# Windowed attention and two MLPs on one core: the second half of the attention taken two rounds at a time, and the weight fold's first blocks moved ahead of the attention's end

## The chip, the cores and the metric

The kernel runs on one core of a Trainium2 chip. The metric is the device time of one execution in microseconds; the lower the better. Three runs of the kernel before gave 868.57 to 869.71 us, with a median of 869.25.

## The reference

```python
def attn(q, k, v):                    # (4 batches, 8 heads, 576 tokens, 64)
    scores = q @ k.transpose(0, 1, 3, 2) / 8
    rel = pos[:, None] - pos[None, :]
    plain   = (rel >= 0) & (rel < 32)                      # heads 0 to 3
    dilated = (rel >= 0) & (rel < 128) & (rel % 4 == 0)    # heads 4 to 7
    return softmax(where(mask, scores, -1e9)) @ v

x = attn(q, k, v) as (2304 tokens, 512)
h = x @ w_in;  x = leaky(h, 0.01) @ w_out                  # 512 -> 2048 -> 512
a, b = x @ w1, x @ w2                                      # 512 -> 1024
out = ((a * b) @ w3) @ w_out2                              # 1024 -> 1024 -> 512
```

q, k and v are float32. The weights arrive as 64-bit floats.

## The kernel before

**Products.** A product of the MLPs is three matmuls (mm3, lines 120 to 122): each operand is held as a high and a low part, and high x high, high x low and low x high are summed in PSUM. A conversion (to_float32, then a split) makes float32 words out of the 64-bit weights first: a scaled copy of the upper words (L107), two on ScalarE (L151, L153), a shift (L141) and an add (L157) on VectorE, then the high part (L110) and the low part (L112).

**MLP 1.** The tokens are cut into seven chunks: two of 320 and 256 tokens for each of batches 0 and 1, then three of 384 for batches 2 and 3 together. A chunk has 16 turns. A turn is one hidden block: 12 matmuls into ps_h (hidden_steps, two PSUM banks in rotation), the leaky step on ScalarE (g, L563), its split (gs: L110 on VectorE, L112 on POOL in the middle chunks) and, two turns later, 12 matmuls into ps_x (project). At the end of a chunk the four accumulators ps_x are copied out to st and stored.

**Attention.** A round is one pair of heads and one part of the tokens, 5 blocks of 64 queries (r = 0) or 4 (r = 1); eight rounds make a batch, 32 in all. A round has these steps: scores (small matmuls into ps_s, L394, then mask, maximum and exponentials, L409 to L418), normalize (L430 to L435), turn_p (transposes into ps_p, L451, copied to pT by ScalarE, L455) and value_steps (small matmuls into ps_o, L472, then copied to x as high and low parts, L500 and L503). For batches 1 to 3 q and k are loaded into "nat" tiles and transposed by VectorE into qT and kT (turn_halves). The tiles ps_s, ps_p and ps_o of the second half share two PSUM banks ("side").

**Order.** Batches 0 and 1 run in an order written out by hand (START). From turn 4 of chunk 2 on, the generator attention() yields steps of rounds 16 to 31, and pace() takes 39/28 of a step in each turn of chunks 2 and 3 and 2.25 in each of the first 13 turns of chunk 4. The text is not the final order: a planner at build time takes, for each engine, the first instruction in the order of the text that its own model holds to be ready. On the chip each engine then runs its list in that order.

**Fold.** w3 and w_out2 are multiplied into one matrix (wp) while MLP 1 goes on. begin_fold, at turn 13 of chunk 4, finishes the attention, closes its pool and opens the pool "fold" in its place; Convert then takes 8 blocks of w_out2 (wo, stored to DRAM) and 16 of w3 (transposed on TensorE, split into w3T), and wp_step makes the products. 1.35 steps of it are taken in each turn from there on. In chunk 6 the blocks of w1 and w2 are converted, and wp is loaded (load_wp) and split. Then come the gates (ps_ab) and the final product (ps_y).

Of the kernel before, what the change touches and what calls it, by code (L numbers as in the profile page):

```python
# [28 lines left out]
def tile_window_attention_two_mlps(  # L29
# [224 lines left out]
    def load_halves(m, src, o):  # L254


        pi, nm = seq[m // 2], "qk"[m % 2]
        t = att.tile([P, NT, D], F32, tag="nat", name=f"{nm}{pi}", bufs=2)
        for g in range(P // E):
            og = o + g // 2 * S * D + g % 2 * E  # L260
            to = t[g * E : (g + 1) * E]
            x = NT * D - E
            nc.sync.dma_start(
                to.rearrange("p n d -> p (n d)")[:, :x], rows(src, og, [[NT * D, E], [1, x]])
            )
        nat_t[nm, pi] = t

    def turn_halves(m):
        pi, nm = seq[m // 2], "qk"[m % 2]
        t = nat_t.pop((nm, pi))  # L270
        dst = att.tile([P, S], F32, tag=nm + "T", name=f"{nm}T{pi}", bufs=2)
        if pair(pi)[2]:
            nc.vector.transpose(dst.rearrange("d (r n) -> d n r", n=NT), t[:, :, :E])
        else:
            for v in range(DILATION):
                us = len(range(v, NT, DILATION))
                other = (NT + v) % DILATION * SR + (NT + v) // DILATION
                to = bass.AP(
                    dst.tensor, dst.offset + v * SR,
                    [list(dst.ap[0]), [1, us], [2 * NT // DILATION, E // 2], [other - v * SR, 2]],  # L280
                )
                at = bass.AP(
                    t.tensor, t.offset + v * D,
                    [list(t.ap[0]), [DILATION * D, us], [2, E // 2], [1, 2]],
                )
                nc.vector.transpose(to, at)
        qk_t[nm, pi] = dst
# [69 lines left out]
    def turn_rows(m):  # L357
        pi, nm = seq[m // 2], "qk"[m % 2]
        plain = pair(pi)[2]
        c = 6 if plain else 8  # L360
        n = S // c
        t = nat_t.pop((nm, pi))
        ps = bank2(f"ps_{nm}T{pi}")
        for g in range(2):
            for c1 in range(c // 2):
                src = t[:n, g * (c // 2) + c1].rearrange("p j d -> p (j d)")
                nc.tensor.transpose(ps[:, g, c1 * n : (c1 + 1) * n], src, ident[:n, :n])
        yield
        dst = att.tile([P, S], F32, tag=nm + "T", name=f"{nm}T{pi}", bufs=2)
        if plain:  # L370
            to = dst.rearrange("d (p g c) -> d g c p", g=2, p=n)
        else:
            to = dst.rearrange("d (c p g) -> d g c p", g=2, p=n)
        copy_on(engine_of[TURN_ON[m]])(to, ps[:, :, : S // 2].rearrange("d g (c p) -> d g c p", p=n))
        qk_t[nm, pi] = dst
        yield
# [134 lines left out]
    def attention(n0, n1):  # L511

        for m in range(n0, n0 + 4):
            transpose_qk(m)
            load_qk(m + 2)
            if m % 2:
                yield
        load_v(n0 // 2 + 1)
        scores(n0)
        yield  # L520
        scores(n0 + 1)
        normalize(n0)
        yield
        for n in range(n0, n1):
            run(turn_p(n))
            normalize(n + 1)
            yield
            if n % 8 != 3:
                scores(n + 2)
                yield  # L530
            transpose_qk(n + 4)
            load_qk(n + 6)
            yield
            if n % 8 == 3:
                scores(n + 2)
                yield
            run(value_steps(n))
            m = n // NA * 4
            if n % NA in (2, 3):
                load_v(m + n % NA)  # L540
            elif n % NA in (5, 7):
                load_v(m + 4 + (n % NA == 7))
            yield


# [119 lines left out]
    def keep_w3(i):  # L665


        def finish(w, e_hi, e_lo):
            ps = bank(f"ps_w3T{i}")
            for j in range(2):  # L670
                for c in range(NG):
                    nc.tensor.transpose(
                        ps[:, (j * NG + c) * P : (j * NG + c + 1) * P],
                        w[:, (c * 2 + j) * P : (c * 2 + j + 1) * P], ident,
                    )
            t = fold.tile([P, 2, 2, NG * P], F32R, tag="w3T", name=f"w3T{i}", bufs=2)
            split(t[:, 0], t[:, 1], ps.rearrange("p (j r) -> p j r", j=2), e_hi, nc.vector)
            w3T.extend((i // (NI // NG), i % (NI // NG) * 2 + j, t[:, :, j]) for j in range(2))

        return finish  # L680

# [23 lines left out]
    wpf = {}  # L705

    def load_wp(ib):
        t = late.tile([P, DM], F32, tag="wpf", name=f"wpf{ib}", bufs=1)
        nc.sync.dma_start(t, wp_dram[ib * P : (ib + 1) * P, :])
        wpf[ib] = t  # L710

# [54 lines left out]

    with ExitStack():
        make_identity(nc, ident)
        att_es, att = pool("att", "right")
        mask_d = masks = att.tile([P, S // QB, KB], BF16, name="masks")  # L770
        nc.vector.memset(masks, 0.0)
        def build_masks():
# [29 lines left out]

        raw_es, rawp = pool("raw", "left")
        homes = {
            "K": (rawp, "kr", 2), "W": (woB_p, "woB", NF // 2), "N": (att, "nat", 2), "V": (att, "v", 2)
        }
        RAW_AT = "WWWWWWWWWWWWWWWWWWWWWWWWNWNWNWNW"
        PAIR_AT = "KKVVKKVVKKVVKKVVKKVVKKVKVKVKVKVK"
# [100 lines left out]
                project(*todo.pop(0))  # L909

        LATE = (4, 13)
        FOLD_PACE = 1.35
        wo2_turn = [0]

# [14 lines left out]
        stream = attention(2 * NA, NR)  # L929
        owed = [0.0]  # L930

        def begin_fold():
            step(*[stream] * 200)
            att_es.close()
            nonlocal fold, fold_es, conv3
            fold_es, fold = pool("fold", "right")
            jobs = [(load_rows, w_out2, jb, keep_wo2(jb)) for jb in range(NI)]
            jobs += [(load_w3, w3, i, keep_w3(i)) for i in range(NI * NI // NG // 2)]

            def fold_tile(tag, dt, bufs):  # L940
                return lambda i: fold.tile([P, 512], dt, tag=tag, name=f"{tag}f{i}", bufs=bufs)

            conv3 = Convert(
                jobs, fold_tile("raw", U64, 2), fold_tile("w", I32, 2), fold_tile("r", I32, 2),
                FOLD_CONV,
            )
            conv3.fetch(2)

        def pace(c):

            owed[0] += 39 / 28 if c < LATE[0] else 2.25
            while owed[0] >= 1:
                owed[0] -= 1
                step(stream)
# [4 lines left out]
        for c, f0, f1 in runs:  # L959
            if first >= f1 - f0:  # L960
                first -= f1 - f0
                continue
            f0, first, f00 = f0 + first, 0, f0
            if c == NCH - 1:
                while conv3.made < len(conv3.jobs) or conv3.done or w3T:
                    fold_step()
                fold_es.close()
                first_es, first_y = pool("first", "right")
                late_es, late = pool("late", "right")

                def raw_last(i):
                    return late.tile([P, 512], U64, tag="raw", name=f"raww{i}", bufs=2)

                wr = {}

                def w_slot(i):
                    wr[i] = late.tile([P, 2, 512], I32, tag="wr", name=f"wr{i}", bufs=2)
                    return wr[i][:, 0]

                jobs = [  # L980
                    (load_cols, (w1, w2)[m], i, keep_cols(w12, (m, i), f"w{m + 1}_{i}"))
                    for i in range(NI)
                    for m in range(2)
                ]
                conv = Convert(jobs, raw_last, w_slot, lambda i: wr[i][:, 1], LAST_CONV)
                conv.fetch(2)
                load_y(0)
            for f in range(f0, f1):
                turn += 1
                mlp1(c, f, f00, f1)  # L990
                if (c, f) == LATE:
                    begin_fold()
                if (c, f) < LATE:
                    pace(c)
                elif c < NCH - 1:
                    owed[0] += FOLD_PACE
                    while owed[0] >= 1:
                        owed[0] -= 1
                        fold_step()
                lagged()  # L1000
                if c == NCH - 1:
                    conv.step()
                    if 2 <= f < 2 + NI:
                        load_wp(f - 2)
                    if 3 <= f < 3 + NI:
                        split_wp(f - 3)
                    if 11 <= f < 11 + NC:
                        split_y(0, f - 11)
# [57 lines left out]
```

## Time and profile before

| | us |
|---|---|
| median of three runs | 869.25 |
| lowest and highest run | 868.57, 869.71 |
| the profiled execution | 868.56 |
| span of its instructions | 866.6 |
| TensorE (PE) busy | 848.2 |
| VectorE (DVE) busy | 346.7 |
| ScalarE (ACT) busy | 352.6 |
| GpSimd (POOL) busy | 210.8 |

The profiled execution lies 1.96 us above its span, and 0.69 us below the median. "Busy" is the time in which an engine executes; PE's matmuls overlap one another, so PE can be busy all the time and still work below its best rate. The distance from one matmul's start to the next one's tells what a matmul costs.

### The profile page before, as it was taken

How to read it: one execution, taken by the hardware profiler on the slowest of the kernel's cores; microseconds unless marked ns; L12 is line 12 of the kernel's file. 1: busy time of each engine (PE TensorE's matmuls, PEld its weight loads, DVE VectorE, ACT ScalarE, POOL GpSimd, SP SyncE). 2: the span in 40 equal slices, each digit the busy share in tenths (PEclk: the TensorE clock that was granted, in tenths of full speed). 3: DMA queues.
4: the chain of work that ended last, by engine and by line, in shares of the span. 5: the costliest groups of instructions: out<-in, count | busy, mean ns of one | idle time of the engine just before them, and what ended most of it. 6: DMA issues, size and time to landing. Idle time of an engine off the chain costs nothing.

```text
span 866.6 us, 14693 instructions
## 1 busy us (share of the span) xinstructions
PE 848.2 (98%) x5774; PEld 772.0 (89%) x5774; DVE 346.7 (40%) x704; ACT 352.6 (41%) x879; POOL 210.8 (24%) x236
## 2 busy tenths in 40 slices
PE   7999998999999999999999999999999999999998
PEld 7799997999999999989899999998888888888887
DVE  4999976344453432274434177731021011000000
ACT  4999945223443343364433175632131121111111
POOL 3311101122322232263222134223123112111110
PEclk9999999999999999999999999999999999999999
DMA  6976575183333311189887575341001000000001
GB/s 152 309 214 231 179 169 137 34 193 73 82 98 92 78 45 50 47 294 349 300 289 236 165 239 155 113 135 49 25 1 61 24 13 13 25 12 13 25 13 48
DMA packets 87333, 103.58 MB, mean 120 GB/s; under 512 B 42849, under 2 KB 65633, under 8 KB 87265
## 3 DMA queue, kind: packets, MB, share of 16 engines
q1 hardware_dynamic: 87264, 102.65, 39.0%
q8 instruction: 45, 0.74, 0.4%
q14 instruction: 24, 0.19, 0.1%
HBM read 85.72 MB, written 16.91 MB: 118 GB/s over the span
## 4 chain that ended last, share of the span: by engine, by line
PE 77%; DMA 7%; DVE 6%; ACT 5%; issue 4%; POOL 2%; SPq 0%; POOLq 0%; DVEq 0%; ACTq 0%
PE ps_ab L120 7%; PE ps_ab L122 7%; PE ps_ab L121 7%; PE ps_x L120 6%; PE ps_x L122 5%; PE ps_x L121 5%; PE ps_h L120 5%; PE ps_h L122 5%; PE ps_h L121 5%; PE ps_y L122 4%; PE ps_y L121 4%; PE ps_y L120 4%; PE ps_s L394 2%; PE ps_o L472 2%; PE ps_wp L122 2%
## 5 line engine op out<-in xcount | busy, mean ns | idle before, releaser
L120 PE MATMUL ps_h<-x,win 128*128 128x384 f32 (+2 forms) x448 | 142.5, 318 | 4.9 <-ACT g L563 4.2
L122 PE MATMUL ps_h<-x,win 128*128 128x384 f32 (+2 forms) x448 | 140.7, 314 | 0.0
L121 PE MATMUL ps_h<-x,win 128*128 128x384 f32 (+2 forms) x448 | 140.4, 313 | 0.0
L120 PE MATMUL ps_x<-gs,wout 128*128 128x384 f32 (+2 forms) x368 | 119.0, 325 | 0.0
L743 DVE TENSOR_TENSOR ab<-a,ps_ab 128x512 f32<-128x512 f32 (+1 forms) x40 | 25.2, 633 | 233.3 <-ACT a L741 225.8
L120 PE MATMUL ps_ab<-ys,w 128*128 128x512 f32 (+1 forms) x320 | 117.7, 368 | 0.6 <-DVE ab L743 0.6
L121 PE MATMUL ps_x<-gs,wout 128*128 128x384 f32 (+2 forms) x368 | 117.7, 320 | 0.1
L122 PE MATMUL ps_ab<-ys,w 128*128 128x512 f32 (+1 forms) x320 | 117.7, 368 | 0.0
L121 PE MATMUL ps_ab<-ys,w 128*128 128x512 f32 (+1 forms) x320 | 117.6, 368 | 0.0
L122 PE MATMUL ps_x<-gs,wout 128*128 128x384 f32 (+2 forms) x368 | 117.4, 319 | 0.0
L112 POOL TENSOR_TENSOR p<-ab,p 128x512 fp32r<-128x512 f32 (+1 forms) x40 | 47.0, 1177 | 211.3 <-ACT p L110 211.3
L110 DVE CAST gs<-g 128x384 fp32r<-128x384 f32 (+2 forms) x92 | 41.3, 449 | 128.9 <-ACT g L563 103.3
L120 PEld LDWEIGHTS ps_h<-x,win 128*128 128x128 f32 x448 | 84.8, 189 | 8.2 <-ACT g L563 6.1
L112 POOL TENSOR_TENSOR gs<-g,gs 128x384 fp32r<-128x384 f32 (+2 forms) x64 | 59.5, 929 | 133.5 <-DVE gs L110 133.5
L563 ACT ACTIVATE g<-ps_h 128x384 f32<-128x384 f32 (+2 forms) x112 | 49.1, 439 | 96.8 <-PE ps_h L122 80.2
L121 PEld LDWEIGHTS ps_h<-x,win 128*128 128x128 f32 x448 | 84.9, 190 | 0.3
L122 PEld LDWEIGHTS ps_h<-x,win 128*128 128x128 f32 x448 | 84.8, 189 | 0.4
L741 ACT COPY a<-ps_ab 128x512 f32<-128x512 f32 (+1 forms) x40 | 21.6, 543 | 139.5 <-PE ps_ab L122 139.5
L120 PEld LDWEIGHTS ps_x<-gs,wout 128*128 128x128 f32 x368 | 69.5, 189 | 1.7
L121 PEld LDWEIGHTS ps_x<-gs,wout 128*128 128x128 f32 x368 | 69.7, 189 | 1.3 <-POOL gs L112 0.4
L122 PEld LDWEIGHTS ps_x<-gs,wout 128*128 128x128 f32 x368 | 69.7, 189 | 0.6
L120 PEld LDWEIGHTS ps_ab<-ys,w 128*128 128x128 f32 x320 | 60.1, 188 | 11.1 <-DVE ab L743 1.0
(109 smaller groups left out, 1553.1 us busy)
## 6 DMA issues: line engine op xcount, KB each, us to landing
wo<-wo_dram SPq DMA_DIRECT2D x32, 512.0 KB
raw<-in_moe_w_in_dram SPq DMA_DIRECT2D x16, 512.0 KB
raw<-in_moe_w_out_dram SPq DMA_DIRECT2D x16, 512.0 KB
rawf<-in_moe_w_dram SPq DMA_DIRECT2D x16, 512.0 KB
raww<-in_moe_w_dram SPq DMA_DIRECT2D x16, 512.0 KB
q<-in_q_dram SPq DMA_DIRECT2D x48, 140.0 KB
k<-in_k_dram SPq DMA_DIRECT2D x48, 140.0 KB
v<-in_v_dram SPq DMA_DIRECT2D x60, 96.0 KB
```

What stands on the lines that cost most here:

```text
L110: copy_on(e_hi)(hi, src)
L112: e_lo.tensor_tensor(lo, src, hi.bitcast(F32), op=ALU.subtract)
L120: nc.tensor.matmul(ps, a[1], b[0], start=first, stop=False)
L121: nc.tensor.matmul(ps, a[0], b[1], start=False, stop=False)
L122: nc.tensor.matmul(ps, a[0], b[0], start=False, stop=last)
L394: nc.tensor.matmul(ps[j * QB : (j + 1) * QB, i - bl.start], qt[d, i * QB : (i + 1) * QB], kt[d, first_key(i, plain) : first_key(i, plain) ...
L472: nc.tensor.matmul(ps[j * D : (j + 1) * D, i * QB : (i + 1) * QB], vt[i][:, h + j, :], t[:, i, j * QB : (j + 1) * QB], start=True, stop=True,)
L563: nc.scalar.activation(g, ps, AF.Prelu, alpha=SLOPE)
L741: nc.scalar.copy(t, ps[0][:, :n])
L743: nc.vector.tensor_tensor(g, t, ps[1][:, :n], op=ALU.mult)
```

## The change

Rounds 16 to 31 are taken in pairs. attention() issues turn_p of round n, then turn_p of round n+1 with the transposes and loads of two q and k tiles, then value_steps of both rounds, then scores and normalize of the next two. There are 36 steps in place of 68, and pace() takes 22/28 and 14/13 of a step per turn in place of 39/28 and 2.25. The loads of v move to the same places of the pairs.

The q and k tiles (nat, qT, kT) get a pool of their own, "qk", that stays open after the attention. The fold's 64-bit words, scaled words and halves take the slots of nat, qT and kT. Its Convert is set up at turn 10 of chunk 4 (CONV_AT), where the first two blocks are asked for, and its first step is taken at turn 13 ahead of begin_fold. The tile w3T is cut in two, each half with its own split, in three buffers of half the size. The tile wpf has two buffers.

```diff
-        t = att.tile([P, NT, D], F32, tag="nat", ...)
+        t = qkp.tile([P, NT, D], F32, tag="nat", ...)      # qT and kT too
...
-        scores(n0)
-        yield
-        scores(n0 + 1)
-        normalize(n0)
-        yield
-        for n in range(n0, n1):
+        for n in (n0, n0 + 1):
+            scores(n)
+        yield
+        for n in (n0, n0 + 1):
+            normalize(n)
+        yield
+        for n in range(n0, n1, 2):
             run(turn_p(n))
-            normalize(n + 1)
             yield
-            if n % 8 != 3:
-                scores(n + 2)
-                yield
-            transpose_qk(n + 4)
-            load_qk(n + 6)
+            run(turn_p(n + 1))
+            turn = [lambda m=m: (transpose_qk(m), load_qk(m + 2)) for m in (n + 4, n + 5)]
+            if n % NA != 4:
+                for f in turn:
+                    f()
             yield
-            if n % 8 == 3:
-                scores(n + 2)
-                yield
-            run(value_steps(n))
+            for i in (n, n + 1):
+                run(value_steps(i))
             m = n // NA * 4
-            if n % NA in (2, 3):
-                load_v(m + n % NA)
-            elif n % NA in (5, 7):
-                load_v(m + 4 + (n % NA == 7))
+            if n % NA == 2:
+                load_v(m + 2)
+                load_v(m + 3)
+            elif n % NA in (4, 6):
+                load_v(m + 2 + n % NA // 2)
+            yield
+            for i in (n + 2, n + 3):
+                scores(i)
+            if n % NA == 4:
+                for f in turn:
+                    f()
+            for i in (n + 2, n + 3):
+                normalize(i)
             yield
...
-            t = fold.tile([P, 2, 2, NG * P], F32R, tag="w3T", name=f"w3T{i}", bufs=2)
-            split(t[:, 0], t[:, 1], ps.rearrange("p (j r) -> p j r", j=2), e_hi, nc.vector)
-            w3T.extend((i // (NI // NG), i % (NI // NG) * 2 + j, t[:, :, j]) for j in range(2))
+            for j in range(2):
+                t = fold.tile([P, 2, NG * P], F32R, tag="w3T", name=f"w3T{i}_{j}", bufs=3)
+                split(t[:, 0], t[:, 1], ps[:, j * NG * P : (j + 1) * NG * P], e_hi, nc.vector)
+                w3T.append((i // (NI // NG), i % (NI // NG) * 2 + j, t))
...
-        t = late.tile([P, DM], F32, tag="wpf", name=f"wpf{ib}", bufs=1)
+        t = late.tile([P, DM], F32, tag="wpf", name=f"wpf{ib}", bufs=2)
...
+        CONV_AT = (4, 10)
...
+        def begin_conv():
+            nonlocal conv3
...
+            def words(tag, dt):
+                return lambda i: qkp.tile([P, 512], dt, tag=tag, name=f"{tag}f{i}", bufs=2)
+
+            conv3 = Convert(jobs, words("nat", U64), words("qT", I32), words("kT", I32), FOLD_CONV)
+            conv3.fetch(2)
...
-            owed[0] += 39 / 28 if c < LATE[0] else 2.25
+            owed[0] += 22 / 28 if c < LATE[0] else 14 / 13
...
+                if (c, f) == CONV_AT:
+                    begin_conv()
                 if (c, f) == LATE:
+                    conv3.step()
                     begin_fold()
```

## Rows read from the trace of the kernel before

**Rows 1.** Windows: stretch, its length, busy us of each engine, PEclk, DMA share, GB/s
```profile
184.00:363.00 179.00, 179.00 (x1644) 169.05 (x1643) 66.90 (x170) 67.44 (x254) 50.38 (x59) 1.00 0.30 76
392.00:500.00 108.00, 107.88 (x581) 98.64 (x580) 40.24 (x68) 39.62 (x68) 25.42 (x30) 1.00 0.78 267
```
**Rows 2.** Timeline of PE: two short bursts among the matmuls of MLP 1
```profile
237.91 0.28 PE L122 MATMUL ps_h<-x,win 128*128 128x256 f32 x1
238.12 1.04 PE L394 MATMUL ps_s<-kT,qT 64*64 64x96 f32 x20
...
239.31 0.28 PE L121 MATMUL ps_h<-x,win 128*128 128x256 f32 x1
239.43 0.29 PE L122 MATMUL ps_h<-x,win 128*128 128x256 f32 x1
239.65 0.69 PE L472 MATMUL ps_o<-pT,v 96*64 96x64 f32 x16
240.26 0.39 PE L120 MATMUL ps_x<-gs,wout 128*128 128x256 f32 x1
240.48 0.28 PE L121 MATMUL ps_x<-gs,wout 128*128 128x256 f32 x1
```
**Rows 3.** Timeline of PE: two rounds' scores in one burst; a longer value burst
```profile
177.50 0.31 PE L122 MATMUL ps_x<-gs,wout 128*128 128x320 f32 x1
177.74 1.54 PE L394 MATMUL ps_s<-kT,qT 64*64 64x96 f32 x32
...
179.46 0.31 PE L121 MATMUL ps_x<-gs,wout 128*128 128x320 f32 x1
179.60 0.31 PE L122 MATMUL ps_x<-gs,wout 128*128 128x320 f32 x1
...
250.62 0.80 PE L472 MATMUL ps_o<-pT,v 96*64 96x64 f32 x20
251.35 0.53 PE L451 MATMUL ps_p<-ident,s 128*96 128x128 f32 x3
```
**Rows 4.** Groups of PE by shape, 184 to 363 us: the scores
```profile
L394 PE MATMUL ps_s<-kT,qT 64*64 64x96 f32 x288 | 15.4, 248 | 0.0
```
**Rows 5.** Timeline of PE where the fold has begun: a wait
```profile
381.87 0.34 PE L122 MATMUL ps_h<-x,win 128*128 128x384 f32 x1
384.26 0.45 PE L120 MATMUL ps_h<-x,win 128*128 128x384 f32 x1 [2.05 <-ACT g L563]
```
**Rows 6.** Windows (columns as in rows 1): right behind that wait
```profile
385.00:390.00 5.00, 5.00 (x22) 5.00 (x21) 4.18 (x6) 2.94 (x6) 3.80 (x4) 0.66 0.95 317
```
**Rows 7.** Timelines of ACT, DVE and POOL ahead of that wait
```profile
381.96 0.62 ACT L110 CAST wo<-wf 128x512 fp32r<-128x512 f32 x1 [2.70 <-DVE wf L157]
...
383.74 0.47 ACT L563 ACTIVATE g<-ps_h 128x384 f32<-128x384 f32 x1
...
377.42 1.22 DVE L110 CAST gs<-g 128x384 fp32r<-128x384 f32 x1 [0.15 <-ACT g L563]
...
379.64 1.24 DVE L141 TENSOR_SCALAR wf<-wf 128x512 int32<-128x512 int32 x1
...
377.08 1.34 POOL L112 TENSOR_TENSOR wo<-wf,wo 128x512 fp32r<-128x512 f32 x1 [1.33 <-ACT wo L110]
```
**Rows 8.** The fold's words: durations in ns (min/median/max), first and last start
```profile
L132 SPq DMA_DIRECT2D rawf<-in_moe_w_out_dram x8: 327/328/433, 340.9 to 380.2; - x8
L141 DVE TENSOR_SCALAR wf<-wf x24: 413/428/1502, 364.1 to 474.6; 128x512 int32<-128x512 int32 x24
```
**Rows 9.** Groups of ACT by shape: the high parts of w3T
```profile
L110 ACT CAST w3T<-ps_w3T 128x512 fp32r<-128x512 f32 x16 | 9.3, 579 | 1.9 <-PE ps_w3T L672 1.9
```
**Rows 10.** Timeline of ACT: exponentials of two blocks
```profile
181.57 0.36 ACT L418 ACTIVATE s<-s,nmax 128x96 f32<-128x96 f32 x1
...
181.93 0.36 ACT L418 ACTIVATE s<-s,nmax 128x96 f32<-128x96 f32 x1
```
**Rows 11.** PE's waits, whole span: waiter, releaser, us in total, times, longest us
```profile
PE ps_h L120 <- ACT g L563: 4.2, 6, 2.1
```

More of the change, by code (lines that the diff above doesn't have):

```diff
@@ L257, in load_halves @@
         pi, nm = seq[m // 2], "qk"[m % 2]
-        t = att.tile([P, NT, D], F32, tag="nat", name=f"{nm}{pi}", bufs=2)
+        t = qkp.tile([P, NT, D], F32, tag="nat", name=f"{nm}{pi}", bufs=2)
         for g in range(P // E):
@@ L270, in turn_halves @@
         t = nat_t.pop((nm, pi))
-        dst = att.tile([P, S], F32, tag=nm + "T", name=f"{nm}T{pi}", bufs=2)
+        dst = qkp.tile([P, S], F32, tag=nm + "T", name=f"{nm}T{pi}", bufs=2)
         if pair(pi)[2]:
@@ L368, in turn_rows @@
         yield
-        dst = att.tile([P, S], F32, tag=nm + "T", name=f"{nm}T{pi}", bufs=2)
+        dst = qkp.tile([P, S], F32, tag=nm + "T", name=f"{nm}T{pi}", bufs=2)
         if plain:
@@ L768, in tile_window_attention_two_mlps @@
         make_identity(nc, ident)
+        qkp_es, qkp = pool("qk", "right")
         att_es, att = pool("att", "right")
@@ L804, in tile_window_attention_two_mlps @@
         homes = {
-            "K": (rawp, "kr", 2), "W": (woB_p, "woB", NF // 2), "N": (att, "nat", 2), "V": (att, "v", 2)
+            "K": (rawp, "kr", 2), "W": (woB_p, "woB", NF // 2), "N": (qkp, "nat", 2), "V": (att, "v", 2)
         }
@@ L930, in tile_window_attention_two_mlps @@
         owed = [0.0]
+        def begin_conv():
+            nonlocal conv3
+            jobs = [(load_rows, w_out2, jb, keep_wo2(jb)) for jb in range(NI)]
+            jobs += [(load_w3, w3, i, keep_w3(i)) for i in range(NI * NI // NG // 2)]
+            def words(tag, dt):
+                return lambda i: qkp.tile([P, 512], dt, tag=tag, name=f"{tag}f{i}", bufs=2)
+            conv3 = Convert(jobs, words("nat", U64), words("qT", I32), words("kT", I32), FOLD_CONV)
+            conv3.fetch(2)
         def begin_fold():
@@ L934, in begin_fold @@
             att_es.close()
-            nonlocal fold, fold_es, conv3
+            nonlocal fold, fold_es
             fold_es, fold = pool("fold", "right")
[L937 to L947, printed above, removed]
         def pace(c):
-            owed[0] += 39 / 28 if c < LATE[0] else 2.25
+            owed[0] += 22 / 28 if c < LATE[0] else 14 / 13
             while owed[0] >= 1:
@@ L967, in tile_window_attention_two_mlps @@
                 fold_es.close()
+                qkp_es.close()
                 first_es, first_y = pool("first", "right")
```

## The prediction

> **What bounds the kernel now.** I read the windows by stage first. From 184 to 363 us, where rounds 16 to 31 run among the turns of chunks 2 to 4, PE is busy for all of 179.00 us at the full granted clock, while DVE, ACT and POOL are each busy for 67 us or less [rows 1]. PE sets the pace there, and a busy PE says nothing of its rate. So I went to PE's timeline and looked at distances from start to start. A 256-column matmul of MLP 1 follows the one before it after 0.12 us (239.31 to 239.43). Around a burst of the attention's small matmuls that step is longer: 0.21 us from the last large matmul to the burst, 0.22 us between the first two large ones behind the value burst [rows 2]. This edge is paid per burst, not per matmul. PE waits for nothing in this stretch that the view of waits would name, so only fewer edges, or fewer matmuls, can shorten it.
>
> Next I asked where PE stands still. The list of PE's waits has one large entry: ps_h waits for the leaky step g, 4.2 us in six places, 2.1 in one of them [rows 11]. The timeline puts that one at 381.87 to 384.26 us [rows 5], in the first microseconds of the fold, and the granted clock right behind it is 0.66 over 5 us [rows 6]: part of that stretch ran at the lower of the two levels. The timelines of the other engines tell why g was late. ACT takes its list in order, and ahead of g at 383.74 stands the cast of a fold block, which waited 2.70 us for DVE; DVE was late since its steps ran long, the shift at 379.64 in 1.24 us [rows 7] where its median is 0.43 [rows 8].
>
> **Part 1: pairs of rounds.** The work on each engine stays the same: the same 16 rounds, matmuls, exponentials and loads. What goes away is edges on PE. First the price of one. From 237.91 to 239.31 lie one score burst of 20 records and two steps of 0.12, so the burst costs 1.40 - 0.24 = 1.16 us in all [rows 2]. Two rounds' scores that happen to run as one burst of 32 records cost 179.46 - 177.50 - 2 x 0.145 = 1.67 us [rows 3]. The difference, 0.51 us for 12 records, is 0.0425 per record, which leaves 1.16 - 20 x 0.0425 = 0.31 us per burst that doesn't depend on its length. For the values: 1.05 - 0.24 = 0.81 us for 16 records [rows 2]; 16 records take 0.61 to the next instruction [rows 2] and 20 take 0.73 [rows 3], so 0.03 each, and 0.81 - 0.48 = 0.33 us is the fixed part.
>
> Now the count. The 288 score records [rows 4] are 16 rounds of 20 or 16. The timeline has them in 16 bursts, and the values of these rounds in 17 (one round is cut in two). If every pair comes out as one burst, 8 and 8 are left: 8 x 0.31 + 9 x 0.33 = 5.5 us less. Against that, in nine places of the trace before a burst already touches the next one (three times scores run into values, six times values into transposes, as at 251.35 [rows 3]), and there about half a fixed part is saved now: 9 x 0.16 = 1.5 us that separate steps would give up, though some new neighbours will form. That is 4.0 to 5.5; I take 4.4, toward the lower end, because a second half can come late for its bank. The bounds of this part are 0 (no pair joins) and -5.5.
>
> Why should the pairs join? Scores of both rounds need both "side" banks, and at the new pace (22/28 of a step per turn, a turn being 24 large matmuls, 2.9 us at 256 columns) a step comes about every 4 to 5 us with its attention share; the copies that free the banks run beside a whole turn of MLP 1. The burst of 32 in [rows 3] shows that the planner does form one. The transposes ps_p show hardly any edge of their own on the timeline, so their split changes nothing.
>
> What is queued behind the longer steps: on ACT, the exponentials of two rounds, one per block every 0.36 us [rows 10], 3.6 us for ten blocks, with g of MLP 1 behind them. PE can go on for 36 matmuls (the other ps_h bank and two projections) before it needs that g: 4.3 us at 256 columns, more in the wider chunks. So this costs nothing alone; it is the third rival below. The loads of v move by less than two rounds, with at least four steps ahead of their use, and on SP nothing stands behind them that PE needs at once; the q and k loads are asked for in twos instead of singly, again two rounds ahead. Both at zero; late, they would hold back a burst, not MLP 1, since the planner puts ready matmuls in front.
>
> **Part 2: the fold's first blocks.** The first loads already leave at 340.9 us [rows 8], so earlier loads are worth nothing by themselves. What moves is the conversion of one block by the text and of two by the buffers: qT and kT come free after the last scores, so scaled copy, ScalarE's two steps, shift and add of these blocks can run while the last rounds still run, and two further blocks can then be fetched. First shift now: 364.1 us [rows 8]. That takes two of the eight blocks of w_out2 out of the stretch in which the wait at 381.87 arose. What the wait costs: 384.26 - 381.87 less a step of 0.17 is 2.2 us, and 5 us at a mean clock of 0.66 [rows 6] lose 1.7, together 3.9. Bounds: 0 (it stays) and -3.9 (it goes). Half the wait would save 1.1 and perhaps the clock's share. I take the middle, -2.0: fewer fold steps stand in front of g, but the same kind of step still does.
>
> **Part 3: the rest.** w3T in halves: 16 more casts and 16 more subtractions. A cast of full width is 0.58 us [rows 9], so a half costs no more than that, at most 16 x 0.58 = 9.3 us more on ACT and about as much on DVE. Both have 40 of 108 us busy in that stretch [rows 1], which covers it; without that cover PE would wait 0.58 us per block, 9 us in all. A gain is bounded by PE's idle time there, 108.00 - 107.88 = 0.12 us [rows 1]. I take 0. The second wpf buffer acts in chunk 6, where PE's remaining waits for g lie: 4.2 - 2.1 = 2.1 us at most is to be had [rows 11], and nothing shows that wpf is what makes g late: 0, bound -1. The pool's new place moves no work.
>
> **The sum.** 868.56 (the profiled execution: span 866.6 and 1.96 around it) - 4.4 - 2.0 = 862.2. The profiled execution lies 0.7 below the median of the runs, so as a median **862.8 us**.
>
> **The rivals.**
> *The wait stays whole.* A shift that could take 0.41 us took up to 1.50 [rows 8], and in the stretch before the wait a DVE step of 1.22 us runs while POOL has one of 1.34 [rows 7]. The fold's blocks bring such pairs of steps in any order. Then only part 1 counts: 869.25 - 4.4 = 864.9. For it: six blocks are still to come at the same rate at the end of chunk 4; against it: two are done. Chance 0.18. (The Trainium skill, SBUF — State Buffer, section "Who interferes with whom", speaks against the change here: GpSimd and those VectorE steps that use both ports hold one port pair in turn, and the second waits for the whole instruction. The long steps of rows 7 agree. By that rule, moving conversions earlier moves the collisions and removes none, and the sum is this rival's.)
> *The pairs come apart.* The change then doesn't do what it says: the planner puts MLP 1's matmuls between the two rounds because the second lacks a bank, as it cut a value burst in two before. With half the pairs joined and the wait whole, 869.25 - 2.2 = 867.0; with none, 869. For it: two banks carry ps_s, ps_p and ps_o. Against: the burst of 32. Chance 0.13.
> *A new wait in one place.* One wait like that of [rows 5] somewhere else takes 3.9 back: 862.8 + 3.9 = 866.7. Chance 0.10.
> *Paired exponentials hold back g: slower.* In chunk 3 PE has 4.3 us of other work; ten exponentials take 3.6; any DVE delay above 0.7 us in front of them makes PE wait. With a wait of 1.5 us and a clock loss of 1.7 each, 3.2 us, and three pairs in chunk 3: 862.8 + 9.6 = 872.4. It decides from two such places on (6.4 us, all of the gain). Against it: PE is never idle from 184 to 363 us now [rows 1]. Chance 0.09.
>
> **How the numbers follow.** The forecast (pairs mostly joined, the wait shortened or gone; its own range 859.5 to 864.5) has 0.50; the rivals have the rest. The range is 859.0 to 868.0: the low end is 869.25 - 5.5 - 3.9 - 1.0, rounded; the high end takes in the whole wait, the new wait and most of the split pairs, and leaves out the slower case and the untouched one. Changes within 0.2% (1.7 us) can't be told from none here. Faster by more: 0.50 + 0.18 + 0.10 and half of 0.13, about 0.83; within: 0.08; slower: 0.09.
>
> **What would show it.** Score bursts of 32 to 40 records and value bursts of the same on PE's timeline, 8 each in place of 16 and 17, with the same edges. The stretch from the first paired scores to the last values shorter by 4 to 5 us with PE still busy throughout. First shift of the fold before the last value burst. At the change from chunk 4 to chunk 5, a wait under 1 us and a clock of 1.00. Wrong would be: bursts of 16 and 20 still; waits of ps_h for g between 184 and 363 us; a second stretch at the lower clock; attention that ends later against chunk 4.

## The result, and the profile after

The changed kernel takes 876.41 us in the median (875.88 to 878.06, 4 runs), the kernel before 868.91 on the same chip: a ratio of 1.0092, 95% interval 1.0072 to 1.0113. It is slower by 7.5 us, where 862.8 was forecast. The profiled execution has a span of 876.2 us, 9.6 longer than before. In the thirteen profiled executions of this case (one for each kernel) chunk 2 begins between 157.4 and 161.2 us, so differences of 2 us between single profiles say little; the stretches below are measured from a chunk's start.

But for one score burst the pairs came out as forecast. The timeline of PE after, from 326 to 372 us, without the matmuls of MLP 1:

```profile
328.35 1.87 PE L394 MATMUL ps_s<-kT,qT 64*64 64x96 f32 x40
337.73 0.71 PE L451 MATMUL ps_p<-ident,s 128*96 128x128 f32 x5
341.95 0.71 PE L451 MATMUL ps_p<-ident,s 128*96 128x128 f32 x5
346.27 1.39 PE L472 MATMUL ps_o<-pT,v 96*64 96x64 f32 x40
351.25 1.54 PE L394 MATMUL ps_s<-kT,qT 64*64 64x96 f32 x32
...
362.02 0.60 PE L451 MATMUL ps_p<-ident,s 128*96 128x128 f32 x4
366.30 0.60 PE L451 MATMUL ps_p<-ident,s 128*96 128x128 f32 x4
370.67 1.15 PE L472 MATMUL ps_o<-pT,v 96*64 96x64 f32 x32
```

Here every score burst and every value burst holds two rounds, 32 to 40 records. Over the whole stretch there are eight value bursts and nine score bursts, since the scores of the first two rounds stayed apart, as they were before:

```profile
199.52 1.04 PE L394 MATMUL ps_s<-kT,qT 64*64 64x96 f32 x20
203.32 0.88 PE L394 MATMUL ps_s<-kT,qT 64*64 64x96 f32 x16
```

The second thing to see in the timeline from 326 to 372 us is the time of its last line. In the kernel before the last value bursts stand here (PE's timeline, 355 to 360 us):

```profile
356.00 0.57 PE L472 MATMUL ps_o<-pT,v 96*64 96x64 f32 x12
359.31 0.34 PE L472 MATMUL ps_o<-pT,v 96*64 96x64 f32 x4
```

The windows from the first ps_h of chunk 2 to that of chunk 5, before and after (stretch, its length, busy time of PE, PEld, DVE, ACT and POOL, granted clock, DMA share, GB/s):

```profile
159.68:371.65 211.97, 211.97 (x1887) 201.71 (x1885) 81.44 (x202) 78.50 (x281) 60.65 (x70) 1.00 0.33 82
```

```profile
160.51:366.65 206.14, 206.14 (x1854) 200.15 (x1853) 77.56 (x198) 76.42 (x276) 58.97 (x68) 1.00 0.32 82
```

The stretch is 5.8 us shorter, with PE busy throughout in both. About 1.3 us of that is the last value burst (1.1 us and its edges), which now falls behind the start of chunk 5; 4.5 us are saved. (Where the last values come ahead of chunk 5, as with the scores ahead of the values below, the same stretch is 207.44 us: 4.5 less without any such correction.) So chunk 5 began early, and everything was lost behind it: from chunk 5's start to the end of the span it is 495.0 us before and 509.6 after, 14.6 more.

The list of PE's waits after shows where (what answers to [rows 11]: waiter, releaser, us in total, times, longest):

```profile
PE ps_w3T L679 <- DVE qTf L157: 7.7, 1, 7.7
PE ps_x L121 <- POOL gs L112: 3.2, 1, 3.2
...
PE ps_x L120 <- ACT st L641: 1.0, 1, 1.0
PE ps_h L120 <- ACT g L570: 0.9, 2, 0.7
```

The wait for g of [rows 5] is gone. In its place PE stands before the first transpose of a w3 block, for whose conversion (qTf) it waits 7.7 us, and before that for gs and for an accumulator. PE's timeline gives the places:

```profile
384.10 0.69 PE L121 MATMUL ps_x<-gs,wout 128*128 128x384 f32 x1 [3.22 <-POOL gs L112]
384.58 0.52 PE L122 MATMUL ps_x<-gs,wout 128*128 128x384 f32 x1
384.90 0.52 PE L120 MATMUL ps_x<-gs,wout 128*128 128x384 f32 x1
...
387.10 0.69 PE L120 MATMUL ps_x<-gs,wout 128*128 128x384 f32 x1 [1.03 <-ACT st L641]
...
391.79 0.34 PE L122 MATMUL ps_x<-gs,wout 128*128 128x384 f32 x1
399.83 1.12 PE L679 MATMUL ps_w3T<-ident,qTf 128*128 128x128 f32 x4 [7.70 <-DVE qTf L157]
```

And the windows after give the clock that went with it (columns as above):

```profile
380.00:390.00 10.00, 5.74 (x20) 4.91 (x19) 4.61 (x6) 5.16 (x9) 4.77 (x5) 0.69 0.90 298
390.00:400.00 10.00, 2.30 (x12) 1.98 (x11) 3.96 (x7) 4.42 (x7) 3.69 (x5) 0.67 0.90 323
400.00:410.00 10.00, 10.00 (x46) 9.44 (x47) 4.01 (x9) 4.85 (x10) 2.89 (x4) 0.78 1.02 389
```

No compute engine is busy for more than 6 of these 10 us while PE waits; the DMA engines are, at 0.90 and above. The three waits are 11.95 us, 9.9 more than the 2.05 before. 22 matmuls of 384 columns follow one another after 0.32 us in place of 0.17, against 10 of them before: with those around them some 2 us more. With the 1.3 us of the value burst this names 13.2 of the 14.6 us; the rest is not traced.

What held the conversions up is seen on POOL and on SP (timelines of both after):

```profile
374.67 1.37 POOL L107 TENSOR_SCALAR qTf<-natf 128x512 f32<-128x512 f32 x2
376.02 1.28 POOL L112 TENSOR_TENSOR gs<-g,gs 128x384 fp32r<-128x384 f32 x1
382.43 0.64 POOL L107 TENSOR_SCALAR qTf<-natf 128x512 f32<-128x512 f32 x1 [5.13 <-DMA natf<-in_moe_w_out_dram]
383.04 1.00 POOL L112 TENSOR_TENSOR gs<-g,gs 128x384 fp32r<-128x384 f32 x1
```

```profile
375.35 1.16 SPq L132 DMA_DIRECT2D natf<-in_moe_w_out_dram  x2
...
391.16 0.38 SPq L654 DMA_DIRECT2D natf<-in_moe_w_dram  x1
```

The loads of the next two blocks leave at 375.35 us, as soon as the conversions at 374.67 have emptied their slots. The first of them is used at 382.43, 7 us later, among the stores of finished blocks. POOL takes its list in order, and behind that conversion stands gs, for which PE waits 3.2 us. The first block of w3 leaves DRAM at 391.16 and reaches PE at 399.83.

### The profile page after: what moved, and what is told of

It reads as the page before. It is cut to its first block, busy times and chain, and to the rows that moved or that the text cites. A ratio compares the mean times of both kernels' runs of the same rounds, so it can differ in the third digit from the quotient of the medians.

```text
span 876.2 us, 14743 instructions
## 1 busy us (share of the span) xinstructions
PE 848.7 (97%) x5774; PEld 776.2 (89%) x5774; DVE 344.5 (39%) x720; ACT 353.2 (40%) x895; POOL 207.7 (24%) x236
## 4 chain that ended last, share of the span: by engine, by line
PE 74%; DMA 7%; issue 6%; ACT 5%; DVE 5%; POOL 2%; SPq 1%; DVEq 0%; POOLq 0%; ACTq 0%
PE ps_ab L120 7%; PE ps_ab L121 7%; PE ps_ab L122 7%; PE ps_x L120 6%; PE ps_x L122 5%; PE ps_x L121 5%; PE ps_h L120 5%; PE ps_h L122 5%; PE ps_h L121 5%; PE ps_y L120 4%; PE ps_y L121 4%; PE ps_y L122 4%; DMA natf<-in_moe_w_dram 2%; PE ps_s L394 2%; PE ps_o L472 2%
## 5 line engine op out<-in xcount | busy, mean ns | idle before, releaser
L110 DVE CAST gs<-g 128x384 fp32r<-128x384 f32 (+2 forms) x92 | 33.8, 367 | 128.9 <-ACT g L570 106.7
```

Of the source, the lines that this page charges most:

```text
L110: copy_on(e_hi)(hi, src)
```

## The experiments

**Theory A.** The fold's blocks can be finished only when the attention's pool closes, that is after the last values. From there to the first transpose of w3 on PE there is work of fixed length: the rest of eight blocks of w_out2 and one of w3, each loaded, converted, split and (w_out2) stored. I call that time the way; it is measured from the first matmul of MLP 1 behind the last value burst. PE's list puts a number of MLP 1's matmuls on it, the cover. Counted on the timeline (ps_h and ps_x between the last ps_o and the first ps_w3T) the cover was 181 before and is 74 now: the last values moved from matmul 315 to matmul 406 behind the start of chunk 4, the first transpose from 496 to 480. PE waits for what the cover lacks. **Rival B.** The conversions moved into the attention, or their buffers in the slots of q and k, make PE wait. **Rival D** (in one run): the way is set by the steps of the conversions on ACT, DVE and POOL and not by the transfers.

**The pairs alone**

```diff
 # the kernel before, with attention() and pace() of the change
-            owed[0] += 39 / 28 if c < LATE[0] else 2.25
+            owed[0] += 22 / 28 if c < LATE[0] else 14 / 13
```

> The pairs of rounds and their pace alone, with the fold, the q and k tiles, w3T and wpf as before. Theory A (the pairs end the attention late against MLP 1's matmuls, so that too few matmuls of MLP 1 are left to cover the eight blocks of w_out2 before PE comes to the first transpose of w3): the attention's matmuls still cost some 4 to 5 us less up to chunk 5, but PE waits again near the first transposes of w3, 3 to 8 us with a stretch at the lower clock; 866 to 876 in all. Rival B (the early conversions on POOL and ACT, or the fold's buffers in the q and k slots, make PE wait): no such wait here, 863 to 866.

Measured: 871.02 us, ratio 1.0039 (1.0025 to 1.0053). One wait at the first transpose, longer than in the whole change:

```profile
399.90 1.11 PE L679 MATMUL ps_w3T<-ident,wf 128*128 128x128 f32 x4 [13.14 <-DVE wf L157]
```

Rival B falls: nothing of the fold is moved here. The way is 33.0 us and the cover 112 matmuls. (Theory A had expected a wait of 3 to 8 us: it has the place right and the size too small.) That this kernel is 5 us faster than the whole change with as much waiting is explained only in part: 2.3 us lie ahead of chunk 2 in its profile, and with one wait in place of three only 7 matmuls of 384 columns follow one another after 0.32 us, in place of 22, which is some 2 us.

**The fold's part alone**

```diff
 # the changed kernel, with attention() and pace() of before
-            owed[0] += 22 / 28 if c < LATE[0] else 14 / 13
+            owed[0] += 39 / 28 if c < LATE[0] else 2.25
```

> The changed kernel with attention() and pace() of before: single rounds, everything else of the change kept. Theory A: the attention ends early again, no wait above 2.5 us at the first transposes of w3; 865 to 870. Rival B: the long wait stays, 873 or more.

Measured: 869.49 us, ratio 1.0019 (1.0008 to 1.0029). The last values are back at matmul 315; cover 152, way 27.0 us, and PE is idle for 0.12 us on it. The long wait comes from the attention. The early conversions do shorten the way, by some 6 us (33.0 to 27.0).

This run also holds the fold's part against the forecast by itself. The wait of [rows 5] is gone here, and the lower clock behind it: from chunk 5's start to 412 us PE is idle for 0.66 us at a granted clock of 1.00, where before it was 2.18 us at 0.96. Yet the kernel is not faster. From 412 to 490 us, where w3 is converted and multiplied, PE is idle for 4.6 us, and before for 0.0. Three entries of its list of waits (whole span; of the first, 1.6 us lie in that stretch):

```profile
PE ps_h L120 <- ACT g L563: 2.5, 4, 1.1
PE ps_w3T L672 <- ACT g L563: 2.0, 2, 1.3
PE ps_wp L120 <- DVE w3T L112: 0.6, 1, 0.6
```

**An earlier pace**

```diff
-            owed[0] += 22 / 28 if c < LATE[0] else 14 / 13
+            owed[0] += 28 / 28 if c < LATE[0] else 8 / 13
```

> The changed kernel with one line changed: 28/28 of a step per turn in chunks 2 and 3 and 8/13 in chunk 4, in place of 22/28 and 14/13, so that the last values come some 130 matmuls of MLP 1 sooner. Theory A: no wait above 2.5 us at the first transposes of w3, and the gain of the pairs is kept: 860 to 866. Rival B: the wait stays, 872 or more.

Here the text lets values of batch 3 be written into x before chunk 3 has read batch 1's from it, so part of x is not the reference's, and the two are tied to each other in a way that the change doesn't have. Measured: 874.60 us, ratio 1.0075 (1.0058 to 1.0093). With a cover of 191 PE is never idle on the way, as theory A has it; but the forecast of 860 to 866 failed, since PE loses 9.4 of the 30 us from 270 on, 6.5 of them in one wait of ps_p for s. The total tells the theories apart no more.

**The fold one, two and three turns later**

```diff
-        LATE = (4, 13)
+        LATE = (5, 0)          # e9: (4, 14); e10: (4, 15)
+        PACED = (4, 13)
...
-            owed[0] += 22 / 28 if c < LATE[0] else 14 / 13
+            owed[0] += 22 / 28 if c < PACED[0] else 14 / 13
```

> The changed kernel with the fold's start moved from turn 13 of chunk 4 to turn 0 of chunk 5, attention and its pace as changed. Theory A: the same late end of the attention, but some 86 more matmuls of MLP 1 ahead of the first transpose of w3: no wait above 2.5 us there, 861 to 867. Rival B: the early conversions are the same, the wait stays, 872 or more.

> The changed kernel with the fold's start at turn 14 of chunk 4 in place of 13, nothing else moved: 122 matmuls of MLP 1 (21 us) between the last values and the first transpose of w3, in place of 74 (13 us). Theory A, with some 28 us for that way: PE waits 4 to 7 us in all between the last values and the first transpose, in place of 12; 866 to 872. If the wait does not depend on this cover, it stays at 11 us or more, 874 to 878.

> The same with the start at turn 15 of chunk 4: 146 matmuls (25 us). Theory A: PE waits 1 to 3 us there; 862 to 867. If the wait does not depend on this cover, 874 to 878.

Measured: 861.69 us, ratio 0.9936 (0.9914 to 0.9958), for turn 0 of chunk 5; 868.23, 0.9999 (0.9989 to 1.0009), for turn 14; 864.69, 0.9961 (0.9947 to 0.9974), for turn 15. The windows from behind the last value burst to the first transpose, for the whole change, turn 14, turn 15 and turn 0 of chunk 5 (the first number is the way, the second PE's busy time on it):

```profile
371.60:399.83 28.23, 16.27 (x82) 15.06 (x79) 15.04 (x24) 13.77 (x24) 12.39 (x13) 0.78 0.84 278
```

```profile
372.30:401.40 29.10, 22.17 (x131) 21.15 (x125) 17.96 (x26) 14.49 (x26) 15.07 (x15) 0.99 0.83 266
```

```profile
371.10:400.00 28.90, 26.55 (x155) 25.20 (x151) 18.28 (x27) 14.98 (x27) 16.08 (x16) 1.00 0.82 274
```

```profile
370.42:399.45 29.03, 28.45 (x168) 27.73 (x165) 18.40 (x28) 15.44 (x28) 16.73 (x17) 1.00 0.85 276
```

The way stays at 28 to 29 us whatever the cover. With 74, 122, 146 and 160 matmuls on it PE is idle for 12.0, 6.9, 2.4 and 0.6 us, and the times go 876.4, 868.2, 864.7 and 861.7. The early conversions and their buffers are the same in all four: the first scaled copies start 18.4 us ahead of the last value burst in each. (At turn 14 the idle time is at the upper edge of what was expected.)

**Half the stores**

```diff
-            nc.sync.dma_start(wo2_dram[jb], t.bitcast(F32))
+            nc.sync.dma_start(wo2_dram[jb][:, 0], t[:, 0].bitcast(F32))
...
-        nc.sync.dma_start(t.bitcast(F32), wo2_dram[jb])
+        for j in range(2):
+            nc.sync.dma_start(t[:, j].bitcast(F32), wo2_dram[jb][:, 0])
```

> The changed kernel, but of each block of w_out2 only the high half is stored to DRAM (256 KB in place of 512), and the high half is read back into both halves, so the product with w_out2 is computed from the wrong low parts; PE's list is unchanged. Theory A says that the eight blocks' traffic (8 x 1 MB in and out, at the 300 GB/s of this stretch some 27 us) is what the first transpose of w3 waits for: with 2 MB less the wait of 7.7 us there falls by some 4 to 7 us, and the time to 868 to 873. Rival D (the conversions' steps on ACT, DVE and POOL set that time, not the transfers): the wait stays at 6 us or more, 874 to 877.

Measured: 872.36 us, ratio 1.0058 (1.0040 to 1.0076). The time lies where theory A put it, the wait does not: PE's wait at the first transpose is 9.1 us, since most of the waiting ahead of it went (10.3 us idle on the way in all, 12.0 with the full stores). The way is shorter by 4 us, 24.2 in place of 28.2. So the stores are one part of it; the DMA share on the way is 0.76 after 0.84. What sets the other 24 us, the loads' own time with two slots or the conversions' steps, is not settled: a third slot for natf wasn't tried. Of the 4 us, 1.6 are idle time of PE; the other 2.4 are matmuls at the full clock instead of the lower (mean clock on the way 0.89 after 0.78).

**Scores ahead of values, and the best of both**

```diff
             yield
-            for i in (n, n + 1):
-                run(value_steps(i))
-            ...                                  # load_v
-            yield
             for i in (n + 2, n + 3):
                 scores(i)
             ...                                  # transposes at n % NA == 4
             for i in (n + 2, n + 3):
                 normalize(i)
             yield
+            for i in (n, n + 1):
+                run(value_steps(i))
+            ...                                  # load_v
+            yield
```

> The changed kernel with the scores of the next pair ahead of the values of this one in attention(); the fold starts where the change has it. The last values come 82 matmuls of MLP 1 sooner and 133 matmuls lie between them and the first transpose of w3, in place of 74. Theory A with the 28 us that the changed kernel took from its last values to that transpose: 133 x 0.173 = 23 us are covered, a wait of 3 to 6 us is left; 865 to 871. Rival B (the early conversions in the slots of q and k make PE wait): 874 or more.

> The order of e6_scores_first and the later fold of e4_fold_later together. Theory A: 217 matmuls, 37 us, cover the 28: no wait at the first transposes of w3, and nothing left to gain over e4_fold_later: 859 to 863. Were the attention's late end itself a cost, it would be 2 us or more faster than e4_fold_later.

Measured: with the fold where the change has it 864.32 us, ratio 0.9951 (0.9930 to 0.9972), slightly better than expected, as PE was idle for only 1.9 of 26.2 us; with the later fold 861.01, ratio 0.9918 (0.9897 to 0.9938). In the second the way is fully covered:

```profile
355.50:393.40 37.90, 37.90 (x227) 37.80 (x223) 21.30 (x33) 20.68 (x37) 20.46 (x21) 1.00 0.82 299
```

Its interval overlaps that of the later fold alone, so no cost of the attention's late end by itself is shown once the fold waits for it; one of some 0.4% isn't excluded. Either of the two beats both kernels.

**The pairs alone with the later fold**

```diff
 # the pairs alone, as above
-        LATE = (4, 13)
+        LATE = (5, 0)
+        PACED = (4, 13)
```

> The pairs of rounds alone (fold, q and k tiles, w3T and wpf as before) with the fold's start at turn 0 of chunk 5. 198 matmuls, 34 us, lie between the last values and the first transpose of w3; e1_pairs_only took 33 us for that way. Theory A: no wait above 2 us there, 860 to 864, the same as e4_fold_later within 0.2%: the moved first blocks, w3T in halves and the second wpf buffer are worth nothing once the cover is enough. Rival: these parts are needed, 866 or more.

Measured: 862.87 us, ratio 0.9950 (0.9933 to 0.9966): the same as with the fold's moved blocks, within the two intervals. Cover 198, way 35.6 us, 0.5 us idle. (The profile is that of the slowest of its ten runs, 867.77 us; 2.1 us of waiting for gs right behind the way, and a lower clock after it, are part of that.)

**w3T in halves and the second wpf buffer alone**

```diff
-            t = fold.tile([P, 2, 2, NG * P], F32R, tag="w3T", ..., bufs=2)
+            for j in range(2):
+                t = fold.tile([P, 2, NG * P], F32R, tag="w3T", ..., bufs=3)
...
-        t = late.tile([P, DM], F32, tag="wpf", ..., bufs=1)
+        t = late.tile([P, DM], F32, tag="wpf", ..., bufs=2)
```

> The kernel before with w3T in two halves of three buffers and two wpf buffers, nothing else. The prediction's part 3 put these at nothing: within 0.2% of before, 866 to 870. If the shorter splits or the second buffer were worth something in chunks 5 and 6: 865 or less; if the 32 additional instructions cost PE time: 871 or more.

Measured: 869.83 us (867.60 to 873.93), ratio 1.0027 (1.0005 to 1.0049). No gain; its interval lies just above 1, so a small loss, up to 0.5%, is likelier than none. Its profile is that of its fastest run and shows where one can lie: from 412 to 490 us PE is idle for 2.1 us in two waits that the kernel before doesn't have:

```profile
PE ps_h L120 <- DVE w3T L112: 1.3, 1, 1.3
PE ps_w3T L672 <- ACT g L563: 0.8, 1, 0.8
```

Of the ten profiles with w3T in halves seven have 0.5 to 4.6 us of such idle time in this stretch (1.5 in the whole change); the three with w3T in one piece have none.

## Why the prediction was wrong

**Part 1, right.** The pairs joined, but for one score burst, and the price per burst held: 4.4 us were forecast, 4.5 measured up to chunk 5. (With seven edges of scores and nine of values the forecast's own terms give 5.1 us, or some 3.7 with its 9 x 0.16 for neighbours taken off; 4.5 lies between.) A score burst of 36 or 40 records fits the 0.31 + 0.0425 per record. Paired exponentials held nothing back: the stretch up to chunk 5 has no idle time on PE, so the rival that ended slower was the wrong one.

**Part 2, the step that failed:** "That takes two of the eight blocks of w_out2 out of the stretch in which the wait at 381.87 arose." The blocks did move: the first shift of the fold is at 353.24 us, ahead of the last value burst. But the step counted what moves ahead of the attention's end and took that end as fixed. Against MLP 1's matmuls it moved back by 91, while the first transpose moved up by 16. The text had the sentence that should have led there: late loads "would hold back a burst, not MLP 1". A late burst holds back the closing of the pool, and so the fold, whose place in PE's list does not follow. Its -2.0 us (the wait for g did go) became +9.9 us of waits and some 2 us of low clock. "Attention that ends later against chunk 4" stood only among the signs of an error, without a price.

Nor did the -2.0 us come where the attention's end stayed in place: the fold's part alone loses the wait for g and its lower clock, as forecast, and gets 4.6 us of waits near w3T for it, at a ratio of 1.0019. That a wait at one place of the fold may come back at another was not among the terms of part 2; the first rival, by which such collisions move and none is removed, comes nearest, but no run shows that collisions make these waits.

Why the attention ends later is read from the bursts shown above. A pair has four hops from PE to another engine and back, one after the other: scores to transposes 9.4 us, to the second transposes 4.2, to the values 4.3, to the next scores 5.0, together 22.9 us. The pace asks for four steps in 4 x 13/14 = 3.7 turns of 4.95 us, 18.4 us, so each pair in chunk 4 falls back by 4.5 us. The fourteen steps of chunk 4 are three and a half pairs, 15.8 us, or at 24 matmuls in 4.95 us some 77 of the 91. The forecast took "a step comes about every 4 to 5 us" from the pace without adding up this chain. With the scores ahead of the values one hop leaves the chain and the values end 82 matmuls sooner; that agrees. What sets the hops can be read in the trace. PE has no idle time in this stretch, and what each of the four bursts needs from the other engines, its operands or its bank, is ready 1.6 to 3.0 us before it starts (normalize ends at 336.16, the copies to pT at 339.01 and 343.23, those to x at 348.64 us). So the place of the bursts in PE's list sets their times; why the planner put them some 21 matmuls apart is not shown.

**Part 3** put the halves at nothing. No gain came, as forecast; but that DVE's and ACT's free time covers the added casts is not borne out: idle time of PE appears near w3T in seven of ten profiles. Whether the halves cause it, by themselves or in the fold's part alone, is not shown; by themselves they lose 0.5% at most.

**The rivals.** That the wait of [rows 5] stays, that the pairs come apart (but for one score burst), and that exponentials hold back g did not come about; new waits in other places did, with some 12 us three times the 3.9 us that one was given. With the fold's start moved to suit, the forecast's number returns, 861.69 and 862.87 us (ratios 0.9936 and 0.9950; 862.8 to 869.25 is 0.9926). That it does so is in part luck: in the second of these kernels no block of the fold is moved, so the reason that part 2 gave plays no role there.

## What to carry to other kernels

Where a pool closes at the end of one phase and its memory opens the next, work out where that end falls against the bound engine's list, not against the clock, and how many of that engine's instructions cover the first transfers behind it. A saving on the bound engine shortens just this cover, so the start of the next phase has to be set again with it. When work is grouped to save edges, add up the chain of hops of one group and hold it against the pace that is asked for.

## What the runs showed of the hardware that was not expected

After a wait the granted clock can cost again as matmuls resume: behind the wait of 7.70 us the window from 400 to 410 us still has a mean clock of 0.78 with PE busy for all of it. Before, an idle time of 2.05 us was followed by 0.66 over 5 us [rows 5, 6]; at turn 15 of chunk 4 PE lost 2.4 us on the way in shorter pieces, and that window's clock is 1.00. A longer wait was not followed by a longer time at the lower level: behind the wait of 2.05 us 10 matmuls of 384 columns follow one another after 0.32 us, behind that of 7.70 us 10, and behind that of 13.14 us (the pairs alone) 7.
